# A table of rank corrections for the first part's order, and a buffer of its own for the second chunk's q

## The chip, the cores and the metric

The kernel runs on one core of one Trainium2 chip. The metric is the time of one execution on the device in microseconds (us); of several runs the median counts.

## The reference, cut to what matters

Attention over keys and values that are averaged in groups of 8, for 8 batches of 576 tokens and 8 heads of 64, and behind it a feed-forward net with a softplus on all 4608 tokens. The weights arrive as float64.

```python
k_p = k.reshape(B, H, S // 8, 8, D).mean(axis=3)
v_p = v.reshape(B, H, S // 8, 8, D).mean(axis=3)
scores = (q @ k_p.transpose(0, 1, 3, 2)) / sqrt(D)
attn = exp(scores - max(scores)); attn = attn / (sum(attn) + 1e-9)
x = (attn @ v_p).transpose(0, 2, 1, 3).reshape(4608, 512)
h = x @ w_in                                  # 512 -> 2048
out = (max(h, 0) + log1p(exp(-abs(h)))) @ w_out
```

## The kernel before

The 4608 tokens are cut into 18 chunks of 256 (two tiles of 128). Each matrix of the feed-forward net is used as a high and a low part (three products for one) on TensorE (PE). w_in and w_out are cut into 16 slices; slice f of both becomes one weight, w0 to w15, which VectorE (DVE) and ScalarE (ACT) convert from the float64 bits.

The program has two parts. The first makes the pooled keys and values of batches 0 and 1 (and 2 for later), converts the 16 weights, does the attention of chunks 0 to 3, and runs chunks 0 to 2 through the net. The second part does the other chunks in a steady pattern, from chunk 4 on with a product scheme that needs fewer products (its operands are the combined w_out, written to DRAM and loaded again by `load_sums`).

In each part the order is planned before anything is issued. Every step is an `Op` with an engine, a cost, the steps that it comes after, and `Slot`s, the buffers that it uses. `Order.run` walks through time: on the engine that could be done first it picks, of the ready steps, the one with the highest rank plus `first`, a correction given with the step. The rank is the cost of the longest chain of steps behind it. Each of the engines then runs its steps strictly in the planned order; a step whose input is late holds all behind it. SyncE (SP) issues all the transfers in one such queue.

Names in what follows: `kps` are the products that pool the keys, `kvlp` those of the last eight keys and values of a batch that don't fill a group of 64, `vps` those of the values; `qTp` transposes q, `sc` are scores, `mn` their minima (keys are scaled by a negative number), `sm` sums, `pm` and `pe` the normalised probabilities (main part and ends), `ptp` and `ltp` their transpositions, `avp` the products with the values. `wst` is a raw slice of w_in or w_out, `wg` a slice in conversion; the conversion is five steps on DVE, a cast on ACT, and a last subtraction on DVE that writes w. `h` are the products with w_in, `acc` and `m` those with w_out.

Chunks 0, 1 and 2 share one memory for q: a tile of chunk 1 can only be loaded when PE has transposed the same tile of chunk 0. `LD` names four load buffers for keys, values and late weights. `spin` hands out tags of a list in turn, whatever slot the plan chose, and the pool `two` alternates on its own for `mn` and `sm`:

```python
def spin(tags, shape, dtype, name):
    tags.append(tags.pop(0))
    return one.tile(shape, dtype, tag=tags[-1], name=name)
...
o_q.append(op(SYNC, 1.4, load,
              [] if c == 0 else [q_free[c - 1, t]] if c < N1 else
              [q_free[c - 1, i] for i in range(T)], lag=2.4))
```

Of the kernel before, what the change touches and what calls it, by code (L numbers as in the profile page):

```python
# [9 lines left out]
F32 = mybir.dt.float32  # L10
# [93 lines left out]
def pooled_attention_softplus_ffn(  # L104
# [41 lines left out]
    def spin(tags, shape, dtype, name):  # L146

        tags.append(tags.pop(0))
        return one.tile(shape, dtype, tag=tags[-1], name=name)

# [90 lines left out]
    def kv(b):  # L241
# [9 lines left out]
        def k_pool(i):  # L251
            if i == 0:
                kp.append(one.tile([SP, H, D], F32, tag="kp", name="kp"))
            tree(st_.pop(("k", i)), kp[0][:, 2 * i:2 * i + 2], engine)
# [7 lines left out]
        def v_pool(i):  # L262
            if i == 0:
                vp.append(one.tile([P, HP, D], F32, tag="vp", name="vp"))
            tree(st_.pop(("v", i)), vp[0][:, 2 * i:2 * i + 2], engine)
# [63 lines left out]
    class Tile:  # L329
# [29 lines left out]

        def least(self, j, ps):  # L360
# [15 lines left out]

        def exp_sum(self, j, ps):
            if j == 0:
                self.sm = two.tile([P, H], F32, tag="sm", name="sm")
# [6 lines left out]
        def sum(self):  # L386
            self.sm = two.tile([P, H], F32, tag="sm", name="sm")
            nc.vector.tensor_reduce(out=self.sm, in_=e_[self.c][:, self.t], axis=AX.X, op=ALU.add)
# [11 lines left out]
        def ends(self):  # L400

            pe = one.tile([P, 7 * R], F32, tag="pe", name="pe")
            self.pe = pe[:, 0:6 * R].rearrange("p (a n r) -> p a n r", a=2, n=3)
# [114 lines left out]

    def copy_out(c, t, tag=None):
        o = one.tile([P, DM], F32, tag=tag, name="o") if tag else spin(O, [P, DM], F32, "o")  # L520
# [186 lines left out]
    def load_wi(c, u):  # L707

        for k in range(2):
# [5 lines left out]

    kinds = {"bank": BANKS, "ld": LD, "ct": ["T0"], "kv": "a", "wg": "ab", "o": "ab", "qT": "ab", "mn": "ab",
             "sm": "ab", "E0": "a", "E1": "a", "pm": "a", "pe": "a", "kp": "a", "vp": "a", "lt_": "a",
             "pT": "a", "g": ["G0", "G1"], "gh": "ab", "gl": "ab", "h": "ab", **{x: "a" for x in late[:NS]}}
# [23 lines left out]
    def weights(f):  # L742
# [5 lines left out]
        def load(i):  # L748
            def fn():
                if early:  # L750
                    if not i:
                        x["raw"] = wpool.tile([P, 2, 4 * 2 * P], I32, tag=late[f % NS], name="wst")
                    st = x["raw"][:, i]
                else:
                    st = x["raw", i] = one.tile([P, 4 * 2 * P], I32, tag=stages[i].name, name="wst")
                if i:
                    nc.sync.dma_start(out=st, in_=wo32[f * P:(f + 1) * P, :])
                else:
                    for r in range(2):
# [4 lines left out]
            return op(SYNC, 1.75, fn, slots=[stages[0 if early else i]], lag=2.2)  # L764

# [16 lines left out]
        def bits(k):  # L782
# [5 lines left out]
            else:  # L788
                g = x["g", k] = spin(O, [P, 1, 4 * P], I32, "wg")
                up = x["raw", k].unsqueeze(1).rearrange("p x (n w) -> p x n w", w=2)[:, :, :, 1]  # L790
# [56 lines left out]
    def batch(b):  # L847
# [24 lines left out]
        o_left = op(SYNC, 1.3, load_left, slots=[ld], lag=2.2)  # L872
        o_k = [op(SYNC, 1.75, load(k, i), slots=[st[i]], lag=2.2) for i in range(2)]
        o_v = [op(SYNC, 1.75, load(v, i), slots=[vt[i] or vt[0]], lag=2.2) for i in range(2)]

# [74 lines left out]
    def attend(c):  # L950
        s_lt, s_pT = Slot("lt_"), Slot("pT")
        lows, e_c = [], []
        tiles = [Tile(c, t) for t in range(T)]
        o_q, subs = [], []
        for t in range(T):
            def load(t=t):
                if 0 < c < N1:
                    qt_[c] = qt_[0]
                elif c not in qt_:
                    new_q(c)  # L960
                load_q_tile(c, t)
            o_q.append(op(SYNC, 1.4, load,
                          [] if c == 0 else [q_free[c - 1, t]] if c < N1 else
                          [q_free[c - 1, i] for i in range(T)], lag=2.4))
        norms = []
        for t, x in enumerate(tiles):
# [5 lines left out]
            o = op(PE, 0.5, lambda x=x, s=s_q: x.qT(bank(s, "qTp")),  # L972
                   [o_q[t], *([av[c - 1]] if c == N1 else [])], [s_q])
            q_free[c, t] = o
            o = op(ACT, act(512), lambda x=x, s=s_q: x.qT_out(s.tile), [o], [s_q, s_qT])
            ends, ss = [], [Slot("bank"), Slot("bank")]
# [3 lines left out]
            for i, s in enumerate(ss):  # L980
                d = op(DVE, 0.46, lambda x=x, i=i, s=s: x.least(i, s.tile), [p, *ends],
                       [s, s_mn])
                if c < N1:
                    def exp_sum(x=x, i=i, s=s, e=s_E[0], t=t):
# [4 lines left out]
                        x.exp_sum(i, s.tile)  # L989
                    ends.append(op(ACT, 1.2, exp_sum, [d], [s, s_mn, s_sm, *s_E], table="exp"))  # L990
# [13 lines left out]
        for x, ends, s_E, s_sm, s_pm, s_pe in norms:  # L1004
            if c == N1:
                ends = [op(DVE, 0.75, x.sum, [ex], [s_sm])]
            o = op(DVE, 1.45, x.norm, ends, [*s_E, s_sm, s_pm, s_pe])
# [21 lines left out]
    def feed(c):  # L1029
# [21 lines left out]
        if c < N1 - 1:  # L1051
            for t in range(T):
                s = Slot("o")
                h = {}

                def copy(t=t, h=h):
                    h["o"] = copy_out(c, t)
                o = op(DVE if t % 2 else ACT, 0.65, copy, [before2], [s, acc_slots[c][t]])
# [73 lines left out]
    for u in range(U1):  # L1132
        combinations(u)
    with tc.manual_schedule(engines={ACT, DVE, PE, SYNC}):
        for o in todo.run():
            o.fn()
# [6 lines left out]
    kinds = {"h": other[:2], "acc": other[2:4], "bank": other[4:], "ld": LD, "q": "a", "pT": "a", "qT": "ab", "lt_": "a",  # L1143
             "pe": "a", "mn": "ab", "sm": "ab", "E": "a", "kp": "a", "vp": "a", "S": "ab", "x": "b",
# [16 lines left out]
    def steady_attention(c):  # L1161
# [8 lines left out]
        for x in tiles:  # L1170
# [4 lines left out]
            qT_done[c].append(o)  # L1175
            o = op(ACT, act(512), lambda x=x, s=s: x.qT_out(s.tile), [o], [s, s_qT])
            last, ss = [], [Slot("bank"), Slot("bank")]
# [3 lines left out]
            for i, s in enumerate(ss):  # L1181
                last = [op(DVE, 0.46, lambda x=x, i=i, s=s: x.least(i, s.tile), [p, *last],
                           [s, s_mn])]
# [8 lines left out]
    def probabilities(c, tiles, s_E, s_lt, subs, where):  # L1192
# [4 lines left out]
        for x in tiles:  # L1197
            s_sm, s_pm, s_pe = Slot("sm"), Slot("G"), Slot("pe")
            o = op(DVE, 0.76, x.sum, [ex], [s_E, s_sm])
            o = op(DVE, 0.38, x.reciprocal, [o], [s_sm])  # L1200
# [189 lines left out]
```

## Time and profile before

| | us |
|---|---|
| median of 3 runs (lowest, highest) | 928.23 (927.97, 931.43) |
| the profiled execution | 930.85 |
| its span, first to last instruction | 929.1 |
| PE busy in the span | 904.6 (97%) |
| DVE busy | 648.6 (70%) |
| ACT busy | 407.3 (44%) |

Busy is the time in which an engine executes at least one instruction. Idle time of an engine counts only where another waits for it. The DMA share is the mean busy share of the core's 16 DMA engines. PEclk is the granted clock of PE as a share of the full one: 1.00 or 0.50, with means between where a stretch holds both.

### The profile page before, as it was taken

What the parts mean: (1) busy time and instruction counts of PE and PEld (TensorE: products, weight loads), DVE (VectorE), ACT (ScalarE), POOL (GpSimd) and SP (SyncE); (2) the same over time, 40 slices, a digit from 0 to 9 for tenths busy, and PEclk for the clock granted to TensorE, in tenths of its full rate; (3) what the DMA queues carried; (4) which work ended last, traced back from release to release, by engine and by line L of the source; (5) the groups of instructions that cost most, each with busy time, mean ns of one, the idle gap of its engine ahead of it and who ended that gap; (6) DMA issues with size and microseconds to landing.
All of it is one profiled execution on the core that took longest, in us unless ns stands there. A gap on an engine that the chain in (4) does not pass through costs nothing.

```text
span 929.1 us, 20504 instructions
## 1 busy us (share of the span) xinstructions
PE 904.6 (97%) x8304; PEld 859.6 (93%) x8304; DVE 648.6 (70%) x1600; ACT 407.3 (44%) x824; POOL 2.4 (0%) x19
## 2 busy tenths in 40 slices
PE   4899999999999999999999999999999999999997
PEld 2678989889899999999999999999999999999997
DVE  4799988868876767777777755777666565747454
ACT  4755433344443534544453435353535344434332
POOL 1000000000000000000000000000000000000000
PEclk9899999999999999999999999999999999999999
DMA  8974636544898678788668865777656566647472
GB/s 231 259 249 147 205 106 182 167 150 136 289 276 239 225 212 256 201 248 233 224 198 248 238 208 186 212 245 214 220 172 216 182 206 186 222 141 227 158 238 78
DMA packets 107085, 191.12 MB, mean 206 GB/s; under 512 B 46064, under 2 KB 60400, under 8 KB 106992
## 3 DMA queue, kind: packets, MB, share of 16 engines
q1 hardware_dynamic: 106992, 189.82, 66.2%
q8 instruction: 65, 1.06, 0.5%
q14 instruction: 28, 0.23, 0.1%
HBM read 167.25 MB, written 22.54 MB: 204 GB/s over the span
## 4 chain that ended last, share of the span: by engine, by line
PE 93%; DVE 3%; DMA 3%; ACT 0%; issue 0%; SPq 0%; DVEq 0%; ACTq 0%
PE h L494 43%; PE m L684 30%; PE acc L516 7%; PE sc L357 3%; PE acc L576 2%; PE avp L461 2%; PE qTp L337 2%; PE avp L468 1%; PE ptp L420 1%; DMA vst<-in_v_dram 1%; PE ltp L432 1%; PE kps L921 1%; DMA kvst<-in_k_dram 1%; DMA kvl<-in_v_dram 1%; DMA wst<-in_moe_w_in_dram 0%
## 5 line engine op out<-in xcount | busy, mean ns | idle before, releaser
L494 PE MATMUL h<-x,w 128*128 128x256 f32 x3456 | 437.8, 282 | 0.7 <-DVE w L822 0.7
L494 PEld LDWEIGHTS h<-x,w 128*128 128x128 f32 x3456 | 422.5, 188 | 4.0 <-DVE w L822 0.9
L543 ACT ACTIVATE g<-h 128x512 f32<-128x512 f32 x120 | 71.7, 598 | 287.0 <-PE h L494 284.7
L684 PE MATMUL m<-w,so 128*128 128x256 f32 x1344 | 177.7, 281 | 0.0
L684 PEld LDWEIGHTS m<-w,so 128*128 128x128 f32 x1344 | 167.4, 188 | 0.0
L684 PE MATMUL m<-w,gh 128*128 128x256 f32 x672 | 133.4, 288 | 0.0
L594 DVE TENSOR_TENSOR sf<-g 128x128 f32<-128x128 f32 x112 | 32.7, 292 | 141.1 <-ACT g L543 140.0
L684 PEld LDWEIGHTS m<-w,gh 128*128 128x128 f32 x672 | 102.2, 188 | 1.9
L684 PE MATMUL m<-w,gl 128*128 128x256 f32 x336 | 94.1, 280 | 0.0
L608 ACT CAST so<-sf 128x512 fp32r<-128x512 f32 x112 | 69.6, 621 | 55.1 <-DVE sf L597 54.6
L613 DVE TENSOR_TENSOR so<-sf,so 128x512 fp32r<-128x512 f32 x112 | 77.3, 690 | 21.9 <-ACT so L608 21.8
L564 DVE TENSOR_TENSOR gl<-g,gh 128x384 fp32r<-128x384 f32 (+1 forms) x120 | 67.3, 560 | 0.7 <-ACT gh L557 0.5
L684 PEld LDWEIGHTS m<-w,gl 128*128 128x128 f32 x336 | 63.1, 188 | 0.0
L516 PE MATMUL acc<-w,g 128*128 128x512 f32 x192 | 60.7, 397 | 0.5 <-ACT g L499 0.5
L557 ACT ACTIVATE gh<-h 128x384 fp32r<-128x384 f32 (+1 forms) x120 | 59.3, 494 | 0.0
L499 ACT ACTIVATE g<-h 128x256 fp32r<-128x256 f32 x96 | 31.6, 382 | 60.7 <-PE h L494 55.6
L705 DVE TENSOR_TENSOR o<-o,m 128x256 f32<-128x256 f32 x98 | 39.7, 418 | 3.9 <-ACT o L697 1.0
L516 PEld LDWEIGHTS acc<-w,g 128*128 128x128 f32 x192 | 34.2, 189 | 6.6 <-ACT g L499 0.7
L364 DVE TENSOR_REDUCE mn<-sc 128x4 f32<-128x288 f32 x72 | 31.1, 450 | 12.2 <-PE sc L357 12.1
L516 PE MATMUL acc<-w,gl 128*128 128x512 f32 x96 | 38.0, 396 | 0.0
L597 DVE TENSOR_TENSOR sf<-g,sf 128x128 f32<-128x128 f32 x112 | 32.7, 292 | 3.9
L406 DVE TENSOR_TENSOR pe<-E,sm 128x96 f32<-128x96 f32 x72 | 15.2, 252 | 26.9 <-PE ltp L432 26.9
(165 smaller groups left out, 933.0 us busy)
## 6 DMA issues: line engine op xcount, KB each, us to landing
w<-wi SPq DMA_DIRECT2D x224, 512.0 KB
out_dram<-o SPq DMA_DIRECT2D x36, 256.0 KB
q<-in_q_dram SPq DMA_DIRECT2D x32, 256.0 KB
wst<-in_moe_w_in_dram SPq DMA_DIRECT2D x32, 256.0 KB
wst<-in_moe_w_out_dram SPq DMA_DIRECT2D x16, 512.0 KB
wi<-w SPq DMA_DIRECT2D x16, 512.0 KB
kst<-in_k_dram SPq DMA_DIRECT2D x24, 288.0 KB
vst<-in_v_dram SPq DMA_DIRECT2D x24, 256.0 KB
```

Source lines behind the costliest of these rows:

```text
L494: nc.tensor.matmul(out=ps[:, 0:CT], lhsT=row(w, kc), rhs=x[:, kc], start=first and kc == j == 0, stop=last and kc == KC - 1 and j == 2)
L499: nc.scalar.activation(out=g, in_=ps[:, 0:CT], func=AF.Softplus)
L516: nc.tensor.matmul(out=accs[c][t], lhsT=a[:, ts], rhs=w, start=f == 0 and j == 0, stop=f == FC - 1 and j == 2)
L543: nc.scalar.activation(out=g, in_=x.rearrange("p (b i) -> p b i", i=P), func=AF.Softplus)
L557: nc.scalar.activation(out=gh, in_=quarters(c, x.rearrange("p (b i) -> p b i", i=P)), func=AF.Softplus)
L564: nc.vector.tensor_tensor(out=gl, in0=quarters(c, g), in1=gh.bitcast(F32), op=ALU.subtract)
L594: tt(out=sf[:, 2], in0=g[:, 0], in1=g[:, 2], op=ALU.add)
L597: tt(out=sf[:, 3], in0=g[:, 3], in1=sf[:, 1], op=ALU.subtract)
L608: nc.scalar.copy(out=so[:, 0], in_=ss[c, u])
L613: nc.vector.tensor_tensor(out=so[:, 1], in0=sf, in1=so[:, 0].bitcast(F32), op=ALU.subtract)
L684: nc.tensor.matmul(out=ms[c][n], lhsT=x, rhs=y, start=u == 0 and j == 0 and n in (1, 6, 5, 4), stop=u == FP - 1 and j == 2 and n in (2, 7, ...
L705: nc.vector.tensor_tensor(out=o, in0=in0, in1=m[n], op=how)
```

## The change

It does four things. The second chunk's q gets one of the four load buffers (slot `s_q1`), held from its load to its transposition; the third chunk uses the first chunk's memory again and waits only for that. The buffers of q's transpositions, outputs, minima and sums take the tag that the plan chose; `spin` and the pool `two` go. In the first part the planner starts with SP at 0.8 and the exponential table loaded, and some loads cost 1.5 instead of 1.75. And a table, `HASTE`, adds a correction to `first` of 110 of the first part's 647 steps, by their number. In the second part the loads of the combined w_out lose their extra rank of 500.

```diff
-    two = ctx.enter_context(tc.tile_pool(name="two", bufs=2))
...
-        def qT_out(self, ps):
-            self.q = spin(Q, [P, HP, P], F32, "qT")
+        def qT_out(self, ps, tag):
+            self.q = one.tile([P, HP, P], F32, tag=tag, name="qT")
...
-                self.mn = two.tile([P, 2, HP], F32, tag="mn", name="mn")
+                self.mn = one.tile([P, 2, HP], F32, tag="mn" + tag, name="mn")
...
+    todo.begin, todo.table = {SYNC: 0.8}, "exp"
...
-        o_k = [op(SYNC, 1.75, load(k, i), slots=[st[i]], lag=2.2) for i in range(2)]
+        o_k = [op(SYNC, 1.5, load(k, i), slots=[st[i]], lag=2.2) for i in range(2)]
...
-        o_q, subs = [], []
+        o_q, subs, s_q1 = [], [], Slot("ld")
...
-                if 0 < c < N1:
+                if c == 1 and c not in qt_:
+                    qt_[c] = one.tile([P, T, H, D], F32, tag=s_q1.name, name="q")
+                elif c == 2:
                     qt_[c] = qt_[0]
...
-                          [] if c == 0 else [q_free[c - 1, t]] if c < N1 else
-                          [q_free[c - 1, i] for i in range(T)], lag=2.4))
+                          [] if c < 2 else [q_free[0, t]] if c < N1 else
+                          [q_free[c - 1, i] for i in range(T)], [s_q1] if c == 1 else [], lag=2.4))
...
+    HASTE = {27: -130, 29: -3, 34: -120, 36: -120, 45: 40, 46: 20, 48: -180, 55: -2, 56: -10,
...
+    for i, x in HASTE.items():
+        todo.ops[i].first += x
...
-               lag=2.4, first=500))
+               lag=2.4))
```

What the plan makes of it, at three places. First SP's queue behind the first chunk's q: transfers in the order of issue, with what an issue waits for (an engine, or, as DMAHW, an earlier transfer). Before, q_143 is the memory shared by the chunks:

```order
L760 DMA wst_152<-in_moe_w_in_dram 128x2x256 x2
L308 DMA q_143<-in_q_dram 128x8x64 [waits DMAHW4_49,DMAHW0_49,PE_49]
L308 DMA q_143<-in_q_dram 128x8x64 [waits DMAHW5_49,DMAHW1_49,PE_49]
L757 DMA wst_152<-in_moe_w_out_dram 128x1024 [waits DMAHW2_49]
L867 DMA kvst_238<-in_k_dram 128x4x256 [waits DMAHW3_49]
L867 DMA kvst_251<-in_v_dram 128x4x256 x2
```

Now, where q_139 is the memory of chunks 0 and 2 and q_237 that of chunk 1:

```order
L753 DMA wst_149<-in_moe_w_in_dram 128x2x256 x2
L750 DMA wst_149<-in_moe_w_out_dram 128x1024 [waits DMAHW0_49]
L302 DMA q_139<-in_q_dram 128x8x64 [waits DMAHW5_49,DMAHW1_49,PE_49]
L860 DMA kvst_225<-in_k_dram 128x4x256 [waits DMAHW2_49]
L302 DMA q_237<-in_q_dram 128x8x64 [waits DMAHW3_49,DVE_49]
L302 DMA q_237<-in_q_dram 128x8x64 [waits DMAHW4_49]
```

The w_out slice has moved ahead of the waits for PE, one tile of chunk 2 stands where two of chunk 1 stood, and chunk 1's two tiles stand behind the keys of batch 1.

Second PE's queue behind the first chunk's scores, down to batch 1's kvlp. Before:

```order
L337 MATMUL qTp<-ident,q 128x128 x8
L921 MATMUL kps<-kvst,zm 64x256 x4
L357 MATMUL sc<-kT_94,qT 64x72 x32
L432 MATMUL ltp<-ident,pe 96x128 x2
L938 MATMUL vps<-kvst,zm 64x128 x16
L921 MATMUL kps<-kvst,zm 64x256 x4
L880 MATMUL kvlp<-kvl,zl 72x512
```

Now, from the same kps on (one qTp of four stands ahead of it):

```order
L914 MATMUL kps<-kvst,zm 64x256 x4
L331 MATMUL qTp<-ident,q 128x128 x8
L351 MATMUL sc<-kT_91,qT 64x72 x16
L424 MATMUL ltp<-ident,pe 96x128 x2
L412 MATMUL ptp<-ident,pm 128x128 x4
L351 MATMUL sc<-kT_91,qT 64x72 x16
L931 MATMUL vps<-kvst,zm 64x128 x16
L424 MATMUL ltp<-ident,pe 96x128 x2
L412 MATMUL ptp<-ident,pm 128x128 x4
L914 MATMUL kps<-kvst,zm 64x256 x4
L331 MATMUL qTp<-ident,q 128x128 x4
L873 MATMUL kvlp<-kvl,zl 72x512
```

Chunk 1's transpositions of q have moved behind kps; both tiles' ltp and ptp of chunk 0 and one more qTp now stand ahead of kvlp. The value products of chunk 0 (avp), which stood behind the scores of chunk 2's first tile, follow right behind this kvlp.

Third DVE's queue down to its copy of batch 1's last keys (`COPY kp`). Before:

```order
L364 TENSOR_REDUCE mn<-sc 128x4 x2
L808 SCALAR_TENSOR_TENSOR wg<-wst,wg 128x1024
L444 TENSOR_TENSOR lt__355<-ltp,lt__355 32x2x128
L813 SCALAR_TENSOR_TENSOR wg<-wst,wg 128x1024
L364 TENSOR_REDUCE mn<-sc 128x4
L889 COPY kp<-kvlp 8x512
```

Now:

```order
L358 TENSOR_REDUCE mn<-sc 128x4
L815 TENSOR_TENSOR w_261<-wg,w_261 128x2x512
L358 TENSOR_REDUCE mn<-sc 128x4
L436 TENSOR_TENSOR lt__353<-ltp,lt__353 32x2x128
L386 TENSOR_SCALAR sm<-sm 128x8
L387 RECIPROCAL sm<-sm 128x8
L391 TENSOR_TENSOR pm<-E,sm 128x512
L398 TENSOR_TENSOR pe<-E,sm 128x96 x2
L882 COPY kp<-kvlp 8x512
```

All of weight 0's conversion (w_261 is w0; its five steps stand further ahead) and three normalisations (rows sm, sm, pm, pe; two of them not shown) are now ahead of the copy; before, one normalisation was, and the last step of weight 0 came later.

## Rows read from the trace of the kernel before

**Rows 1.** The page's opening line.

```profile
span 929.1 us, 20504 instructions
```

**Rows 2.** Busy time by stages: busy us of each engine, granted clock, DMA share, GB/s.

```profile
14.80:34.00 19.20, 13.95 (x140) 9.69 (x140) 11.39 (x24) 11.56 (x57) 0.00 (x0) 0.82 0.92 246
34.00:82.00 48.00, 41.60 (x432) 34.97 (x433) 44.02 (x90) 33.41 (x98) 0.00 (x0) 0.96 0.73 231
82.00:179.00 97.00, 97.00 (x624) 88.07 (x623) 85.90 (x149) 35.79 (x89) 0.00 (x0) 1.00 0.52 165
179.00:300.00 121.00, 120.23 (x1041) 110.28 (x1040) 90.95 (x211) 54.97 (x103) 0.00 (x0) 1.00 0.70 220
300.00:924.20 624.20, 624.01 (x5991) 612.50 (x5990) 410.52 (x1119) 267.47 (x474) 0.00 (x0) 1.00 0.67 207
```

(The busy times are those of PE, PE's weight loads, DVE, ACT and POOL, in this order.)

**Rows 3.** Timeline of PE: start, duration, work, [idle before, released by].

```profile
15.38 0.63 PE L337 MATMUL qTp<-ident,q 128*128 128x128 f32 x4 [0.58 <-DVE mn L364]
17.66 0.63 PE L337 MATMUL qTp<-ident,q 128*128 128x128 f32 x4 [1.66 <-DMA q<-in_q_dram]
20.69 3.64 PE L921 MATMUL kps<-kvst,zm 128*64 128x256 f32 x8 [2.40 <-DMA kvst<-in_k_dram]
```

**Rows 4.** Timeline of SP's queue: start and duration of the issues.

```profile
6.10 1.73 SPq L760 DMA_DIRECT2D wst<-in_moe_w_in_dram  x2
12.24 1.54 SPq L308 DMA_DIRECT2D q<-in_q_dram  x2
13.84 0.57 SPq L757 DMA_DIRECT2D wst<-in_moe_w_out_dram  x1
14.46 0.42 SPq L867 DMA_DIRECT2D kvst<-in_k_dram  x1
```

**Rows 5.** Timeline of DVE.

```profile
18.84 0.69 DVE L791 TENSOR_SCALAR wg<-wst 128x1024 int32<-128x1024 int32 x1 [2.00 <-DMA wst<-in_moe_w_out_dram]
...
20.18 0.16 DVE L392 TENSOR_SCALAR sm<-sm 128x8 f32<-128x8 f32 x1
...
21.22 0.42 DVE L406 TENSOR_TENSOR pe<-E,sm 128x96 f32<-128x96 f32 x2
...
25.54 0.46 DVE L364 TENSOR_REDUCE mn<-sc 128x4 f32<-128x288 f32 x1 [3.29 <-PE sc L357]
...
31.86 0.69 DVE L889 COPY kp<-kvlp 8x512 f32<-8x512 f32 x1 [1.51 <-PE kvlp L880]
...
38.22 1.22 DVE L822 TENSOR_TENSOR w<-wg,w 128x1024 fp32r<-128x1024 f32 x1
```

**Rows 6.** Timeline of PE, 32 to 79 us.

```profile
32.09 1.04 PE L337 MATMUL qTp<-ident,q 128*128 128x128 f32 x8
...
36.56 0.76 PE L357 MATMUL sc<-kT,qT 64*64 64x72 f32 x27 [1.37 <-ACT kT L225]
...
37.21 1.94 PE L461 MATMUL avp<-pT,vs 64*64 64x256 f32 x15
...
43.01 0.40 PE L432 MATMUL ltp<-ident,pe 128*96 128x128 f32 x2 [1.21 <-DVE pe L406]
...
51.74 0.40 PE L432 MATMUL ltp<-ident,pe 128*96 128x128 f32 x2 [1.44 <-DVE pe L406]
...
78.08 0.40 PE L432 MATMUL ltp<-ident,pe 128*96 128x128 f32 x2 [1.46 <-DVE pe L406]
```

**Rows 7.** Busy time by stages, short stretches (columns as in rows 2).

```profile
20.00:22.00 2.00, 1.31 (x4) 0.75 (x5) 1.93 (x7) 1.08 (x4) 0.00 (x0) 0.50 1.09 359
20.70:26.70 6.00, 6.00 (x74) 3.82 (x74) 2.14 (x6) 0.99 (x6) 0.00 (x0) 0.50 1.19 269
37.00:40.40 3.40, 3.40 (x42) 2.42 (x36) 3.00 (x5) 3.34 (x19) 0.00 (x0) 0.50 1.02 334
```

**Rows 8.** Batch 1's values: timelines of SP's queue and of PE.

```profile
34.20 1.58 SPq L867 DMA_DIRECT2D kvst<-in_v_dram  x2
...
43.77 2.57 PE L938 MATMUL vps<-kvst,zm 128*64 128x128 f32 x32
```

More of the change, by code (lines that the diff above doesn't have):

```diff
@@ L251, in k_pool @@
         def k_pool(i):
-            if i == 0:
+            if not kp:
                 kp.append(one.tile([SP, H, D], F32, tag="kp", name="kp"))
@@ L375, in less, with exp_sum @@
                     [P, 2, 2, SP]), op=ALU.subtract)
-        def exp_sum(self, j, ps):
+        def exp_sum(self, j, ps, tag):
             if j == 0:
-                self.sm = two.tile([P, H], F32, tag="sm", name="sm")
+                self.sm = one.tile([P, H], F32, tag="sm" + tag, name="sm")
             for m in range(HP):
@@ L384, in exp_sum, with sum @@
                                      accum_out=self.sm[:, h:h + 1])
-        def sum(self):
-            self.sm = two.tile([P, H], F32, tag="sm", name="sm")
+        def sum(self, tag):
+            self.sm = one.tile([P, H], F32, tag="sm" + tag, name="sm")
             nc.vector.tensor_reduce(out=self.sm, in_=e_[self.c][:, self.t], axis=AX.X, op=ALU.add)
@@ L400, in ends @@
         def ends(self):
-            pe = one.tile([P, 7 * R], F32, tag="pe", name="pe")
-            self.pe = pe[:, 0:6 * R].rearrange("p (a n r) -> p a n r", a=2, n=3)
+            self.pe = one.tile([P, 2, 3, R], F32, tag="pe", name="pe")
             for a in range(2):
@@ L517, in ffn2, with copy_out @@
                                  start=f == 0 and j == 0, stop=f == FC - 1 and j == 2)
-    def copy_out(c, t, tag=None):
-        o = one.tile([P, DM], F32, tag=tag, name="o") if tag else spin(O, [P, DM], F32, "o")
+    def copy_out(c, t, tag):
+        o = one.tile([P, DM], F32, tag=tag, name="o")
         if t % 2 == 0:
@@ L763, in fn @@
                                 "(g r p) f -> r p g f", r=2, p=P)[r])
-            return op(SYNC, 1.75, fn, slots=[stages[0 if early else i]], lag=2.2)
+            return op(SYNC, 1.5, fn, slots=[stages[0 if early else i]], lag=2.2)
         loads = [load(i) for i in range(2)]
@@ L788, in bits @@
             else:
-                g = x["g", k] = spin(O, [P, 1, 4 * P], I32, "wg")
+                g = x["g", k] = one.tile([P, 1, 4 * P], I32, tag=gslot[k].name, name="wg")
                 up = x["raw", k].unsqueeze(1).rearrange("p x (n w) -> p x n w", w=2)[:, :, :, 1]
@@ L872, in batch @@
         o_left = op(SYNC, 1.3, load_left, slots=[ld], lag=2.2)
-        o_k = [op(SYNC, 1.75, load(k, i), slots=[st[i]], lag=2.2) for i in range(2)]
-        o_v = [op(SYNC, 1.75, load(v, i), slots=[vt[i] or vt[0]], lag=2.2) for i in range(2)]
+        o_k = [op(SYNC, 1.5, load(k, i), slots=[st[i]], lag=2.2) for i in range(2)]
+        o_v = [op(SYNC, 1.5, load(v, i), slots=[vt[i] or vt[0]], lag=2.2) for i in range(2)]
         s_left, s_kp, s_vp = Slot("bank"), Slot("kp"), Slot("vp")
@@ L972, in attend @@
             o = op(PE, 0.5, lambda x=x, s=s_q: x.qT(bank(s, "qTp")),
-                   [o_q[t], *([av[c - 1]] if c == N1 else [])], [s_q])
+                   [o_q[t], *([av[c - 1]] if c == N1 else [])], [s_q, *([s_q1] if c == 1 else [])])
             q_free[c, t] = o
-            o = op(ACT, act(512), lambda x=x, s=s_q: x.qT_out(s.tile), [o], [s_q, s_qT])
+            o = op(ACT, act(512), lambda x=x, s=s_q, n=s_qT: x.qT_out(s.tile, n.name), [o], [s_q, s_qT])
             ends, ss = [], [Slot("bank"), Slot("bank")]
@@ L980, in attend, with exp_sum @@
             for i, s in enumerate(ss):
-                d = op(DVE, 0.46, lambda x=x, i=i, s=s: x.least(i, s.tile), [p, *ends],
+                d = op(DVE, 0.46, lambda x=x, i=i, s=s, n=s_mn: x.least(i, s.tile, n.name), [p, *ends],
                        [s, s_mn])
                 if c < N1:
-                    def exp_sum(x=x, i=i, s=s, e=s_E[0], t=t):
+                    def exp_sum(x=x, i=i, s=s, e=s_E[0], t=t, n=s_sm):
                         if c == 0 and 0 not in e_:
@@ L988, in exp_sum @@
                         x.slot = e.name
-                        x.exp_sum(i, s.tile)
+                        x.exp_sum(i, s.tile, n.name)
                     ends.append(op(ACT, 1.2, exp_sum, [d], [s, s_mn, s_sm, *s_E], table="exp"))
@@ L1005, in attend @@
             if c == N1:
-                ends = [op(DVE, 0.75, x.sum, [ex], [s_sm])]
+                ends = [op(DVE, 0.75, lambda x=x, n=s_sm: x.sum(n.name), [ex], [s_sm])]
             o = op(DVE, 1.45, x.norm, ends, [*s_E, s_sm, s_pm, s_pe])
@@ L1054, in feed, with copy @@
                 h = {}
-                def copy(t=t, h=h):
-                    h["o"] = copy_out(c, t)
+                def copy(t=t, h=h, s=s):
+                    h["o"] = copy_out(c, t, s.name)
                 o = op(DVE if t % 2 else ACT, 0.65, copy, [before2], [s, acc_slots[c][t]])
@@ L1175, in steady_attention @@
             qT_done[c].append(o)
-            o = op(ACT, act(512), lambda x=x, s=s: x.qT_out(s.tile), [o], [s, s_qT])
+            o = op(ACT, act(512), lambda x=x, s=s, n=s_qT: x.qT_out(s.tile, n.name),
+                   [o], [s, s_qT])
             last, ss = [], [Slot("bank"), Slot("bank")]
@@ L1181, in steady_attention @@
             for i, s in enumerate(ss):
-                last = [op(DVE, 0.46, lambda x=x, i=i, s=s: x.least(i, s.tile), [p, *last],
+                last = [op(DVE, 0.46, lambda x=x, i=i, s=s, n=s_mn: x.least(i, s.tile, n.name), [p, *last],
                            [s, s_mn])]
@@ L1198, in probabilities @@
             s_sm, s_pm, s_pe = Slot("sm"), Slot("G"), Slot("pe")
-            o = op(DVE, 0.76, x.sum, [ex], [s_E, s_sm])
+            o = op(DVE, 0.76, lambda x=x, n=s_sm: x.sum(n.name), [ex], [s_E, s_sm])
             o = op(DVE, 0.38, x.reciprocal, [o], [s_sm])
```

11 lines of the change are left out of this document (4 added, 7 removed), and 12 rows, old and new, of the table HASTE.

## The prediction

> **What bounds the kernel now.** I read the page's opening line first, then the busy time by stages, since a share over the whole span hides where time is lost. [rows 1, 2] The span is 929.1 us. From 82 to 179 us PE is busy 97.00 of 97.00 us, and from 300 to 924.2 us 624.01 of 624.20: there nothing but less PE work would help, and the change leaves the number of PE's instructions as it is. What can be won lies ahead of 82 us: from 14.8 to 34 PE is busy 13.95 of 19.20 us, from 34 to 82 41.60 of 48.00, idle 5.25 and 6.40.
>
> The second view is the timeline of PE and, for who is late, of SP and DVE. PE's scores of the first chunk end at 14.80 (15.38 less the 0.58 of idle time). Then it waits 0.58, 1.66 and 2.40 us, and only at 20.69 do the products of the second batch's keys (kps) start [rows 3]. The last two waits are for transfers. SP shows why: it is free at 7.83, but stands until 12.24, because its next two loads write the second chunk's q over the first chunk's and must wait for PE's transpositions; the w_out half of the first weight and the keys queue behind, at 13.84 and 14.46 [rows 4]. DVE in turn waits for that w_out until 18.84, then 3.29 us for scores [rows 5]. In 14.8 to 34 it is busy only 11.39 of 19.20 us; from 34 to 82 it is at work 44.02 of 48.00 [rows 2], and PE's idle pieces there end mostly on it: 1.21, 1.44, 1.46 us for DVE's pe; 1.37 is for the keys that ACT scales [rows 6]. So DVE leaves time unused early and has none later.
>
> The third view is the granted clock in short stretches. After the 4.64 us of waits PE runs at 0.50 from 20.7 to 26.7, and once more from 37 to 40.4, behind 1.37 us of waiting [rows 7]. PE is fully busy in both, so half of 6.0 and of 3.4 us is lost: 3.0 and 1.7. The Trainium skill (TensorE: Matmul & The Clock Gate, section "What's actually happening") has two levels, 1.2 and 2.4 GHz, idle sending PE to the lower and busy work back; the rows agree.
>
> **The change, part by part.** *The start of the queue.* With a buffer of its own the second chunk's q needn't wait for the first's transpositions. In the new order the w_out half goes out right behind w_in, at 7.9 rather than 13.84, into a queue that was empty. One q tile still waits for PE (a tile of the third chunk, which does overwrite); the old pair of such loads was out by 13.78 [rows 4], so this one is too, and the key half stands right behind: 13.85 instead of 14.46, 0.6 earlier. Ahead of it in the transfers are 0.75 MB less (one q tile of 0.25 MB, the w_out half of 0.5 MB); at the 359 GB/s of 20 to 22 us [rows 7] that is 2.1 us. Together 2.7, so kps could start at 18.0. Against it: PE has then transposed one q tile where it had two, half of the 1.04 us of eight such [rows 6], so the lead in work is 2.2; and the scores behind kps now wait for ACT's copy of a tile transposed only just before. No row has that wait; its bounds are 0 and the 0.58 of PE's own small wait at 15.38 [rows 3]; I take 0.3, nearer to the middle since the second tile's transposition lies over part of it. **(a) 1.9 us**; bounds 0.3 (if the transfers gain nothing but SP's 0.6, less 0.3) and 2.2.
>
> *The clock.* PE's idle stretch ahead of kps shrinks from 4.64 to some 3 us. Whether that spares it the first slow stretch no row shows: between 0 and 3.0. I take 0.6, near nothing, because the longest wait stays long. The second stretch came behind the 1.37 us; the new order puts the first chunk's value products, 1.94 us of them in the slow stretch [rows 6], ahead of those scores instead of behind them, so PE has work while ACT is late. I take all 1.7; bounds 0 and 1.7. **(b) 2.3 us.** At full clock throughout, (b) would be 4.7.
>
> *The table.* It moves work between stages on DVE and PE. At the row where DVE copies the second batch's left-over keys (31.86 before, released by PE's kvlp [rows 5]), the new order has ahead of it two more normalisations, one more minimum and the last step of weight 0. A normalisation runs from 20.18 to 21.64, 1.46 us; the minimum is 0.46, the last step 1.22 [rows 5]: 2 x 1.46 + 0.46 + 1.22 = 4.6 us. PE has eight more qTp, eight ptp (the same form) and two ltp ahead of that kvlp: 1.04 + 1.04 + 0.26 = 2.3 us [rows 6]. With a lead of 1.9 + 0.6 = 2.5, PE reaches kvlp at about the old time, and by then DVE is 4.6 us ahead of its old self. That is possible, since it idled 7.8 us in 14.8 to 34; what makes it possible is the w_out that lands while DVE has nothing else.
>
> From 34 to 82 PE lives on what DVE hands it. PE's lead, (a) plus (b), is 4.2; DVE's 4.6 carries it and leaves 0.4. On top the order may close part of DVE's own 3.98 idle us there; the bounds are nothing and all of it. I take a third, 1.3, because the same engine hands work back and forth with ACT and PE and every hand-over can make a new wait. **(c) 1.7 us**; bounds 0, and the 6.40 that PE idles.
>
> *What costs nothing.* Pools replaced by tags, the smaller pe tile, and names bound at planning add no instruction. A wait that the old rotation of buffers could have caused beyond 300 us would show as PE idle, and there is 0.19 us of it. The loads of the combined w_out lose their rank and fall a few rows back in SP's queue; they are hidden by PE's full queue (179 to 300: 120.23 of 121.00 busy), and if that cover were gone each would cost PE a transfer's delay. The correction of SP's start and of the load costs only shifts the plan.
>
> **Sum.** 1.9 + 2.3 + 1.7 = 5.9 us. The profiled execution took 930.85 (span 929.1, 1.75 around it), 2.62 above the median of 928.23. So I expect 924.95 for one like the profiled one, and for the median 922.3, 0.64% less. What this kernel's measurement can tell from no change is about 0.5%, 4.6 us; below 923.6 counts as faster.
>
> **Rivals.** *The transfers stay the bound.* In 14.8 to 34 the DMA share is 0.92 [rows 2]: moving one load forward moves another back. For it: SP's loads from 14.46 on are the same bytes. Against it: the empty stretch from 7.83 to 12.24. Then only (a) remains and waits reappear later: 926.3. Chance 0.16.
>
> *The clock falls as before.* (b) is gone, 928.2 - 3.6 = 924.6. For it: a wait of some 3 us stays ahead of kps. The same page of the Trainium skill says that the gate runs free of the kernel's start, so the point at which it falls differs from run to run; by that rule one trace can't promise (b), and the time would be this one. Chance 0.10.
>
> *More than that.* DVE's lead also removes the waits in its name, and PE stays at full clock: 1.9 + 4.7 + 5.0 of the 6.40 = 11.6, 916.6. Against it: the new order has its own hand-overs. Chance 0.12, spread from 916 to 920.
>
> *Slower: the second batch's values come late.* The second chunk's q takes one of four load buffers, so those values wait for a buffer, and the second half stands behind the fourth chunk's q, which waits for PE. In the old order they were out by 35.78 and used at 43.77 without a wait, at most 8.0 us [rows 8]. In the new order their last issue comes after PE's qTp beside kvlp, about 32.5, landing by 40.5; PE gets there at about 39.5. A us of lateness costs one, since all behind stands in PE's order: 1 us is likely harmless within (c), landing at 45.4 uses up the gain, at 50.0 the kernel is slower by 0.5%. Chance 0.06 for no gain or a loss (930 to 934).
>
> **Numbers.** The forecast's case, 920.0 to 924.7, has 0.56, of which 0.46 below 923.6. The range 919.0 to 927.0 leaves out part of the first and third rivals and all of the fourth, about 0.19. Faster: 0.46 + 0.12 = 0.58. Same: 0.10 + 0.16 + 0.10 + 0.01 = 0.37. Slower: 0.05.
>
> **What would show it.** In the new trace kps of the second batch starts near 18.0, not 20.7; DVE starts weight 0 near 15; the granted clock has one slow stretch, not two; the first product with weight 0 (right behind the values' products, which end at 46.34 before [rows 8]) starts between 41.5 and 43; PE's idle from 34 to 82 is about 3.5 us; from 82 on it is full. I'm wrong if kps starts after 20, if the values of the second batch hold PE, or if PE's busy stretch after 82 has new holes.

## The result and the profile after

The changed kernel took 920.6 us (median of 4 runs, 919.36 to 922.68), the kernel before 928.88 in the same measurement (4 runs, 927.97 to 931.43): a ratio of 0.9909, interval 0.9879 to 0.9938. In the two later groups of runs, in which each kernel ran more often, the kernel before had 930.12 (16 runs, 927.52 to 935.84) and 930.77 (21 runs, 927.73 to 935.71), the changed kernel 919.88 (6 runs, 919.24 to 921.73) and 919.59 (5 runs, 919.2 to 921.84): ratios of 0.9878 [0.9844, 0.9912] and 0.9871 [0.9852, 0.989]. So the gain is 8.3 us by the first measurement and 10.2 and 11.2 by the larger ones. In these the changed kernel's runs also lie closer together, 2.5 and 2.6 us apart instead of 8.3 and 8.0, though they are fewer; in the first, with four runs each, it was 3.3 and 3.5.

The opening line of its page and its busy time by stages, as in [rows 1, 2]:

```profile
span 920.9 us, 20496 instructions
```

```profile
14.80:34.00 19.20, 15.76 (x170) 10.57 (x162) 14.66 (x33) 16.03 (x75) 0.00 (x0) 0.82 0.99 260
34.00:82.00 48.00, 45.76 (x466) 38.92 (x459) 45.09 (x88) 30.72 (x86) 0.00 (x0) 1.00 0.73 231
82.00:179.00 97.00, 97.00 (x628) 87.17 (x627) 90.02 (x158) 37.59 (x89) 0.00 (x0) 1.00 0.53 176
179.00:300.00 121.00, 121.00 (x1081) 112.84 (x1080) 91.84 (x217) 54.16 (x102) 0.00 (x0) 1.00 0.70 218
300.00:916.00 616.00, 616.00 (x5903) 604.92 (x5901) 402.69 (x1097) 265.42 (x470) 0.00 (x0) 1.00 0.68 208
```

PE idles 3.44 us from 14.8 to 34 (5.25 before), 2.24 from 34 to 82 (6.40 before), and not at all from 82 to 916, where it had 0.77 and 0.19 [rows 2]. That is 1.81 + 4.16 + 0.96 = 6.9 us. PE's busy time as a whole fell by another 1.1 us, from 904.6 to 903.5. Together 8.0 of the 8.2 between the two spans.

Its timeline of PE, SP's queue and DVE at the places of [rows 3 to 6, 8]:

```profile
16.71 0.63 PE L331 MATMUL qTp<-ident,q 128*128 128x128 f32 x4 [1.74 <-DMA q<-in_q_dram]
19.04 3.64 PE L914 MATMUL kps<-kvst,zm 128*64 128x256 f32 x8 [1.71 <-DMA kvst<-in_k_dram]
...
36.45 0.72 PE L351 MATMUL sc<-kT,qT 64*64 64x72 f32 x30 [0.23 <-ACT kT L219]
37.80 0.40 PE L424 MATMUL ltp<-ident,pe 128*96 128x128 f32 x2 [0.62 <-DVE pe L398]
...
40.32 2.57 PE L931 MATMUL vps<-kvst,zm 128*64 128x128 f32 x32
42.82 1.68 PE L486 MATMUL h<-x,w 128*128 128x256 f32 x12
```

```profile
7.86 0.47 SPq L750 DMA_DIRECT2D wst<-in_moe_w_out_dram  x1
13.49 0.37 SPq L302 DMA_DIRECT2D q<-in_q_dram  x1
13.91 0.58 SPq L860 DMA_DIRECT2D kvst<-in_k_dram  x1
...
33.55 2.51 SPq L860 DMA_DIRECT2D kvst<-in_v_dram  x1
```

```profile
15.39 0.68 DVE L784 TENSOR_SCALAR wg<-wst 128x1024 int32<-128x1024 int32 x1
...
28.48 1.23 DVE L815 TENSOR_TENSOR w<-wg,w 128x1024 fp32r<-128x1024 f32 x1
```

The w_out half goes out at 7.86 instead of 13.84, and DVE begins weight 0 at 15.39 instead of 18.84 and ends it at 29.7 instead of 39.4 [rows 4, 5]. The waits of 1.2 to 1.5 us for DVE's pe are down to 0.62 and less. The values of the second batch are there when PE comes to them (no bracket at 40.32).

The granted clock, stretches that answer to [rows 7]:

```profile
17.80:24.20 6.40, 5.16 (x16) 3.23 (x16) 4.65 (x9) 3.74 (x18) 0.00 (x0) 0.50 1.08 297
36.00:41.00 5.00, 3.67 (x78) 2.74 (x80) 4.83 (x13) 3.56 (x15) 0.00 (x0) 1.00 0.88 249
```

One slow stretch is left of two.

How far PE is ahead by then can be read at one row that all the kernels have: the first product m (of the scheme that is used from chunk 4 on). In the kernel before, and in the changed one:

```profile
258.14 0.40 PE L684 MATMUL m<-w,gh 128*128 128x256 f32 x2
```

```profile
251.09 0.40 PE L676 MATMUL m<-w,gh 128*128 128x256 f32 x2
```

So 7.05 of the 8.2 us are won ahead of this row. In the two later profiles of the changed kernel it stands at 249.90 and 250.25.

### The profile page after: what moved, and what is told of

The parts are those of the page before. It is cut to its first block, busy times and chain, and to the rows that moved or that the text cites. A ratio compares the mean times of both kernels' runs of the same rounds, so it can differ in the third digit from the quotient of the medians.

```text
span 920.9 us, 20496 instructions
## 1 busy us (share of the span) xinstructions
PE 903.5 (98%) x8304; PEld 858.8 (93%) x8304; DVE 649.9 (71%) x1600; ACT 407.8 (44%) x824; POOL 2.4 (0%) x19
## 4 chain that ended last, share of the span: by engine, by line
PE 95%; DVE 2%; DMA 1%; SPq 1%; ACT 0%; issue 0%; DVEq 0%; ACTq 0%
PE h L486 44%; PE m L676 31%; PE acc L508 7%; PE acc L568 2%; PE sc L351 2%; PE avp L453 2%; PE qTp L331 2%; PE ptp L412 1%; PE avp L460 1%; DMA wst<-in_moe_w_out_dram 1%; PE ltp L424 1%; DMA kvl<-in_v_dram 1%; SPq L302 0%; ACT E L376 0%; DVE o L697 0%; DVE wg L806 0%
```

## The experiments

Three groups, each with the kernel before on the same chip. In the first the kernel before took 930.23 (17 runs), nearly as in the other two, so its times can be set beside the 919.6 to 919.9 of the changed kernel, which did not run in it.

**Without the table.**

```diff
-    for i, x in HASTE.items():
-        todo.ops[i].first += x
```

> The changed kernel without the table of corrections; the second chunk's own buffer for q, the named buffers and the planner's new costs stay. Theory A (most of the 8 us comes from the new order on DVE and PE from 34 us on, of which the table is the cause): most of the gain goes, ratio to the kernel before 0.996 to 1.000, PE idle from 34 to 82 us 5 us or more. Rival B (the gain is the earlier start of the queue, which the buffer alone gives): ratio 0.991 to 0.994.

929.48 us (12 runs), ratio 0.999 [0.9976, 1.0004]: the whole gain is gone. But the profile doesn't show it where the table was thought to work. The stages 34 to 82 and 179 to 300, and PE's waits in the second:

```profile
34.00:82.00 48.00, 44.13 (x441) 37.30 (x433) 44.71 (x86) 31.05 (x88) 0.00 (x0) 1.00 0.70 228
...
179.00:300.00 121.00, 117.02 (x1017) 108.00 (x1015) 88.34 (x207) 53.82 (x100) 0.00 (x0) 1.00 0.72 217
```

```profile
286.49 0.66 PE L331 MATMUL qTp<-ident,q 128*128 128x128 f32 x4 [0.72 <-DVE x L470]
287.69 0.66 PE L331 MATMUL qTp<-ident,q 128*128 128x128 f32 x4 [0.54 <-DVE x L470]
299.85 1.08 PE L351 MATMUL sc<-kT,qT 64*64 64x72 f32 x32 [2.19 <-DVE E L365]
```

In 14.8 to 82 us PE idles 4.83 + 3.87 = 8.7, three us less than before (3.87 from 34 to 82, where 5 or more were expected); in 179 to 300 it idles 4.0, three more. Its first m stands at 253.43, 4.7 us ahead of the kernel before, and at the end only 1.5 of them are left (span 927.6). The size came as expected and the reason did not.

The plan shows how the table reaches so far: the second part is planned from the state in which the first ends. Without the table the second part's order on PE, DVE and ACT is step for step that of the kernel before; with it, 21 of PE's 415 places and 55 of SP's 209 hold another step.

**The second chunk's q in shared memory again**, with the table kept and the plan made anew:

```diff
-                if c == 1 and c not in qt_:
-                    qt_[c] = one.tile([P, T, H, D], F32, tag=s_q1.name, name="q")
-                elif c == 2:
+                if 0 < c < N1:
                     qt_[c] = qt_[0]
...
```

> The changed kernel with the table, but the second chunk's q again in the first chunk's memory; the plan is made anew with the same table. Theory A: the start of the queue is lost (about 2 us, the keys of the second batch after 20 us) and what the table does later stays in part, ratio 0.994 to 0.998. Rival B: nothing is left without the buffer, ratio 0.998 to 1.002.

924.83 us (6 runs), 0.9942 [0.9927, 0.9956], as expected: 5 us over the changed kernel. The products of the second batch's keys start at 20.41, behind three waits for transfers (1.04, 1.75, 2.13), nearly as in [rows 3]; from 179 to 300 us PE doesn't wait. The w_out half goes out late too, at 13.28, and DVE starts weight 0 at 18.87, so the 5 us are not the keys' alone.

**The w_out half late**: on SP behind the second chunk's q, and DVE's first steps of weight 0 behind its minima; all else as changed.

```diff
+    behind(41, 269)      # SP: weight 0's w_out half behind the second chunk's q
+    behind(42, 249)      # DVE: its first step behind a minimum
...
+    behind(43, 42)
```

> The changed kernel's order, with one transfer later: the w_out half of the first weight is issued behind the keys and the second chunk's q, as late as in the kernel before, and DVE's first two steps on that weight stand behind the scores' minima. Everything else keeps its place. Theory A (DVE's lead, made by a w_out that lands while DVE has nothing else): DVE starts the weight at 18 to 20 us instead of 15.4, PE idles 3 to 5 us more before 60 us, ratio 0.994 to 0.997. Rival B (the keys' arrival and the clock): less than 0.6 us, ratio 0.990 to 0.992.

926.12 us (6 runs), 0.9952 [0.9937, 0.9967], as expected: 6 us over the changed kernel. PE's timeline shows the price, DVE late by the work that it could not do early:

```profile
27.23 0.66 PE L424 MATMUL ltp<-ident,pe 128*96 128x128 f32 x2 [3.95 <-DVE pe L398]
```

But the edit does more than take the lead away. The half is issued at 15.21 and DVE starts weight 0 later than in the kernel before (18.84) and than the 18 to 20 us that were expected:

```profile
21.30 0.69 DVE L784 TENSOR_SCALAR wg<-wst 128x1024 int32<-128x1024 int32 x1 [5.89 <-DMA wst<-in_moe_w_out_dram]
```

The normalisation that PE waits for stands behind all five steps on this weight, in an order made for an early w_out, and the granted clock from 14.8 to 34 us is 0.73 where it was 0.82. So 6 us is what this order loses without the early transfer, and not what the lead gives over the kernel before.

**The rank of the loads put back** (one of the edits costed at nothing):

```diff
-               lag=2.4))
+               lag=2.4, first=500))
```

> The changed kernel with the old rank of 500 for the loads of the combined w_out in the second part. All theories so far: within 0.5 us of the changed kernel, ratio 0.990 to 0.992. If the 0.8 us of PE's idle time that went away between 179 and 300 us is this edit's, 0.8 us slower than the changed kernel and that idle time is back.

925.1 us (6 runs), 0.9941 [0.9925, 0.9956]: a miss, 5 us. The rank changes more than SP's queue here: the plan of the second part comes out otherwise on PE (45 of 415 places), DVE and ACT too. Its profile has a hole in the stretch that the prediction took as full, and SP's queue says why:

```profile
253.57 3.08 PE L486 MATMUL h<-x,w 128*128 128x256 f32 x24 [2.77 <-DMA w<-wi]
```

```profile
245.55 1.02 SPq L520 DMA_DIRECT2D out_dram<-o  x2
246.68 0.94 SPq L657 DMA_DIRECT2D w<-t  x2
247.68 1.86 SPq L704 DMA_DIRECT2D w<-wi  x4
249.58 2.01 SPq L242 DMA_DIRECT2D kst<-in_k_dram  x2
```

The slices of w_in for that product go out at 247.68, behind loads of the combined w_out (`w<-t`); the changed kernel has a pair of them out here:

```profile
244.94 1.04 SPq L704 DMA_DIRECT2D w<-wi  x2
```

**The changed kernel again, and three edits beside it.** Its measure in this group:

> The changed kernel once more, as the measure for the other three of this group. Every theory expects 920 to 923 us, a ratio of 0.990 to 0.993.

919.88 us, as told above. The first edit keeps PE's clock up by extra transposes in the two waits for transfers:

```diff
+            for _ in range(14 if (self.c, self.t) == (2, 1) else 0):
+                nc.tensor.transpose(out=ps[:, 0:P], in_=ident, identity=ident)
...
+                for _ in range((0, 13)[b] if i == 0 else 0):
+                    nc.tensor.transpose(out=bank(s_k, "kps")[:, 0:P], in_=ident, identity=ident)
```

> The changed kernel with 14 extra transposes ahead of the transposes of the second chunk's second q tile, and 13 ahead of the second key/value batch's first pooled product, written into the same PSUM tiles and overwritten; they fill the two waits of 1.74 and 1.71 us for transfers. Nothing of the computation is left out. Theory C (the slow stretch of TensorE's clock that follows these waits still costs the changed kernel 1 to 2.5 us): the stretch is gone and the time is 1 to 2.5 us under the changed kernel's. Rival (what PE does there hangs on ACT's and DVE's hand-overs, not on its own speed): within 0.6 us of the changed kernel, and the waits for ACT and DVE behind it grow by what PE saves.

921.05 us (6 runs), 0.9884 [0.985, 0.9918], no better than 919.88. The clock did stay up; 16 to 34 us here:

```profile
16.00:34.00 18.00, 16.14 (x181) 11.48 (x180) 13.93 (x32) 15.27 (x69) 0.00 (x0) 1.00 1.03 278
```

against this in the unedited kernel of the same group:

```profile
16.00:34.00 18.00, 16.74 (x161) 11.32 (x162) 13.69 (x31) 15.03 (x68) 0.00 (x0) 0.81 1.04 271
```

The waits have moved rather than gone: one of 0.79 us for q appears at 30.70, and the keys' products wait 0.75 where they waited 0.57. At the first m 0.6 us is left (249.32 against 249.90). The run doesn't price the clock, since the extra transposes are 3.3 us of PE's time themselves (1.75 and 1.58).

The second puts the first half of the second batch's keys ahead of chunk 2's q tile, on SP and PE. (The expectation names two tiles; the edit passes one.)

```diff
+    ahead(23, 302)       # SP: first half of batch 1's keys ahead of chunk 2's q tile
+    ahead(33, 310)       # PE: its products ahead of that tile's transposes
```

> The changed kernel with one more step of the start put forward: on SP the first half of the second batch's keys ahead of the second chunk's second and third q tiles, and on PE the pooled product of these keys ahead of those tiles' transposes. If the wait for these keys is a loss of its own (step (a) of the prediction, us for us): the pooled product starts 1 to 3 us earlier and the time falls by 1.5 to 3 us. Rival (the q tiles come as much later, and ACT and DVE, which work on their scores, wait instead): within 0.7 us of the changed kernel.

920.75 us (6 runs), 0.9888 [0.9856, 0.992], no gain, though its PE timeline has the products 3.4 to 4.1 us earlier than the profiles of the changed kernel, and without a wait:

```profile
14.90 1.94 PE L914 MATMUL kps<-kvst,zm 128*64 128x256 f32 x8
17.06 0.63 PE L331 MATMUL qTp<-ident,q 128*128 128x128 f32 x4 [0.22 <-DVE wg L789]
18.25 0.63 PE L331 MATMUL qTp<-ident,q 128*128 128x128 f32 x4 [0.56 <-DMA q<-in_q_dram]
19.23 0.63 PE L331 MATMUL qTp<-ident,q 128*128 128x128 f32 x4 [0.36 <-DMA q<-in_q_dram]
21.65 1.24 PE L351 MATMUL sc<-kT,qT 64*64 64x72 f32 x32 [1.78 <-ACT qT L338]
```

The wait has moved to DVE's, q's and ACT's names, as the rival said, and the first m stands at 249.91, where it did.

The third is the rank's removal alone, in the kernel before (the diff of the rank above, the other way round):

> The kernel before with one edit of the change alone: the rank of 500 taken from the loads of combined w_out; 22 rows move in SP's queue, none on PE, DVE or ACT. If that rank costs by itself the 3 us that the run with the rank put back into the changed kernel lost: 926 to 927 us, a ratio of 0.996 to 0.998. Rival (it costs only with the list that the planner makes behind the new first part, where a slice of w_in comes late): as the kernel before, within 0.6 us, a ratio of 0.9993 to 1.0007.

931.66 us (12 runs, 927.76 to 936.14), 1.0009 [0.9988, 1.003]: by itself it is worth nothing, the rival's case. The profiled execution was the longest of the twelve, 936.14 us, and gave the clue to the rest. Up to 285 us it stands where the kernel before stands; then DVE waits for a key and two value loads of the fourth batch, and PE for DVE:

```profile
287.30 1.14 DVE L212 TENSOR_TENSOR kst<-kst 72x512 f32<-72x512 f32 x2 [2.77 <-DMA kst<-in_k_dram]
294.23 1.15 DVE L212 TENSOR_TENSOR vst<-vst 128x512 f32<-128x512 f32 x2 [2.14 <-DMA vst<-in_v_dram]
300.02 1.15 DVE L212 TENSOR_TENSOR vst<-vst 128x512 f32<-128x512 f32 x2 [4.32 <-DMA vst<-in_v_dram]
```

```profile
305.11 1.08 PE L357 MATMUL sc<-kT,qT 64*64 64x72 f32 x32 [2.98 <-DVE E L371]
```

In the profiled execution of the kernel before, which was shorter, PE's wait at this place was 0.17. Behind the waits the clock falls once more:

```profile
306.50:309.90 3.40, 3.40 (x19) 3.40 (x18) 1.73 (x5) 0.89 (x2) 0.00 (x0) 0.50 0.50 146
```

PE's waits here are 3.9 us (0.39, 0.54 and 2.98) for 0.4 in the kernel before, and half of 3.4 us goes to the clock: 3.5 + 1.7 = 5.2 of the 5.3 us between the two spans (934.4 and 929.1). The two are different programs, but by the medians the edit between them is worth nothing, and both have runs from under 928 to some 936 us. So it is likely, though not shown on one program, that this place differs by 3 us and more between executions. It is also the one that undid the run without the table.

**Where the loads of the fourth batch stand.** That gave theory L: these loads land too late, and part of the gain is that the changed kernel's list has them earlier. Three edits touch SP's order alone, in the second part; the changed kernel ran beside them.

> The changed kernel once more, on the chip of the other three of this group, as their measure. Every theory expects 919 to 923 us, a ratio of 0.987 to 0.993.

919.59 us. First, the kernel before with these loads early:

```diff
+    ahead(305, 142)      # next chunk's q tile, eight slices of w_in earlier
+    ahead(274, 248)      # keys of the fourth batch, one pair earlier
+    ahead(278, 258)      # values, one pair earlier
+    ahead(280, 289)
```

> The kernel before with one edit in the second part, on SP alone: the next chunk's q tile eight w_in slices earlier, and of the fourth key/value batch one load of keys and both loads of values one pair of w_in slices earlier. No row moves on PE, DVE or ACT. Theory L (at 285 to 305 us these loads land too late for DVE and so for PE, by an amount that differs from run to run, and part of the change's gain is that its list places them earlier): PE's waits at 290 to 302 us are gone, the time is 1 to 3 us under the kernel before and its runs lie closer together. Rival (all of the gain lies in the first 82 us): within 0.7 us of the kernel before.

928.32 us (10 runs, 927.48 to 930.2), 0.9969 [0.9953, 0.9985]: 2.5 us less in the median, and no run is longer than 930.2; the shortest one is as before (927.48 and 927.73). So the edit takes away what the worse executions lose.

Not all of the 2.5 is the loads'. In its profile the first m stands at 255.86, 2.3 us ahead already, though the edit leaves the first part as it was: the second slow stretch of the clock is missing there. Behind this row it gains 0.5 more (span 926.3). Of its ten runs 7 have a mean granted clock of 0.996 or more, of the 21 of the kernel before 6. Among these the medians are 928.01 and 929.09, among the others 929.46 and 931.84: 1.1 to 2.4 us at a like clock.

The same four lines in the kernel without the table:

> The changed kernel without its table (as in the first group) and with the early loads. Without the table the profile showed PE idle for 8.7 us in 14.8 to 82 us, 3.0 us less than in the kernel before, and for 4.0 us in 179 to 300 us, 3.2 more, which cancelled. Theory L: the second of these goes, 925 to 927 us, a ratio of 0.994 to 0.997; what then is left to the changed kernel, 5 to 6 us, is what the table is worth in the first 82 us with what follows from it. Rival (the table alone carries the gain): 929 us, as without the table.

925.05 us (6 runs), 0.9928 [0.9911, 0.9945]: 4.4 us under the kernel without the table. Its first 82 us had been better all along, and the late loads had eaten it: the first m stands at 253.10, 5.0 us ahead of the kernel before, and at the end it is 5.7 (span 923.4), where 4.7 had become 1.5.

Last, the changed kernel with the loads where the kernel before has them:

```diff
+    ahead(305, 248)
+    ahead(274, 258)
+    ahead(278, 289)
```

> The changed kernel with the opposite edit, on SP alone: the same q tile and the same loads of the fourth batch put back to the places that they have in the kernel before, between the same w_in slices. Theory L: PE waits 0.4 to 4 us for DVE or ACT at 275 to 300 us, and the time is 1 to 4 us over the changed kernel. Rival: within 0.7 us of it.

928.42 us (12 runs, 923.4 to 931.28), 0.9964 [0.9946, 0.9983]: 8.8 us over the changed kernel, more than twice the most that was expected. Of the three loads two change their place among the slices of w_in, the next chunk's q tile and the first values of the fourth batch; the keys come out where they stood. So four fifths of the gain hang on the places of two loads in SP's queue; nothing else differs. The execution with a profile was the shortest of the twelve; of the others there is no trace. Even it shows DVE late by these values, PE's wait for DVE, and the stretch around it with the DMA engines full (share 1.03):

```profile
280.30 1.16 DVE L206 TENSOR_TENSOR vst<-vst 128x512 f32<-128x512 f32 x2 [2.59 <-DMA vst<-in_v_dram]
```

```profile
283.95 0.66 PE L331 MATMUL qTp<-ident,q 128*128 128x128 f32 x4 [1.75 <-DVE x L470]
```

```profile
265.00:285.00 20.00, 18.25 (x161) 17.39 (x161) 14.71 (x40) 7.92 (x16) 0.00 (x0) 1.00 1.03 259
```

The kernel before and then the changed kernel in the same stretch:

```profile
265.00:285.00 20.00, 20.00 (x172) 20.00 (x171) 14.42 (x40) 10.74 (x17) 0.00 (x0) 1.00 0.96 273
```

```profile
265.00:285.00 20.00, 20.00 (x179) 19.36 (x178) 15.67 (x41) 8.69 (x17) 0.00 (x0) 1.00 0.94 253
```

Its first m stands at 249.88, so the lead was there, and 0.8 us of it is lost behind it (span 921.7). The other runs must lose far more. Part of it may be the clock: at the medians their mean granted clock is 0.994, the changed kernel's in this group 1.000. A stretch like the one behind the waits of the rank alone, 3.4 us at half, takes 0.002 off such a mean, so by estimate it would be about three such stretches more, 5 us. Where they lie no trace shows.

In group 3 the chain is then: 930.77 before; 928.32 with its loads early; 925.05 with the change's other edits but no table; 919.59 with the table and the list that follows from it. That is 2.5, 3.3 and 5.5 us. The three are worth this in this order; they aren't independent, and some of the first is the clock, as told above.

## Why the prediction was right, and where it was not

The time (920.6 for a forecast of 922.3) lies in the range; the gain was 8.3 us in that measurement, and 10.2 and 11.2 in the larger ones, where the sum had 5.9. Most of the marks that were to show it did: DVE starts weight 0 at 15.39 (near 15), one slow stretch of the clock instead of two, the first product with weight 0 at 42.82 (41.5 to 43), the values without a wait, full from 82 us on. That this early gain was kept is luck as far as the prediction goes: it hung on two loads of the second part, which the prediction doesn't name. Step by step:

(a), *the start of the queue*: the keys' products start at 19.04, 18.32 and 18.66 in the three profiles of the changed kernel, 1.65 to 2.4 us earlier, for a forecast of 18.0 and 2.7. The mechanism is the one described, SP's empty stretch. But that a still earlier start is worth its own length is refuted for the changed kernel: with the products at 14.90 the time didn't fall. What sharing the memory costs (5 us, the second experiment) is more than (a); there DVE's start on weight 0 is late as well (18.87), so that run doesn't price (a) alone.

(b), *the clock*: reckoned as in the prediction, half of PE's busy time at 0.50, 5.16 / 2 = 2.6 us is left of 4.7, a saving of 2.1 where 2.3 was put. PE's busy time as a whole fell by 1.1. The run with the rank put back shows what the stretch that is left costs: its first part is that of the changed kernel, step for step, and its profile has the full clock there.

```profile
14.80:34.00 19.20, 15.46 (x174) 10.87 (x174) 16.28 (x37) 17.28 (x79) 0.00 (x0) 1.00 1.15 286
```

```profile
248.16 0.40 PE L676 MATMUL m<-w,gh 128*128 128x256 f32 x2
```

This first m is 1.7 to 2.9 us ahead of the three profiles of the changed kernel. In the 15 runs of the changed kernel the time goes the same way: the four with a mean granted clock of 0.995 or 0.996 took 921.6 to 922.68 us, ten of the others 919.2 to 919.91, one 921.84. So the size in the sum was sound. What it had wrong is to count on it: how much of a run is slow differs from execution to execution (a mean granted clock of 0.991 to 0.998 in the runs of the kernel before). The kernel before with its loads early has the same first part as the kernel before, and its profile has a clock of 1.00 from 34 to 82 us, where that of the kernel before has 0.96. The Trainium skill (TensorE: Matmul & The Clock Gate, "What's actually happening") has it that the gate isn't tied to the kernel's start, and these two profiles agree. The prediction gave that a rival's chance and took all of the second stretch into the sum.

(c), *the table and DVE's lead*: the mis-sized term. PE's idle time from 34 to 82 us was to fall from 6.40 to some 3.5 and fell to 2.24, and 1.81 us went from the stage before it; the sum had 1.7 for all that DVE would give. From the first product with weight 0 to the first m the lead over the kernel before grows by 3.6 us, in each of the three profiles of the changed kernel. That the new order lives on DVE's early work is shown by the third experiment: with a late w_out it loses 6 us and has one wait of 3.95 for DVE. That run overstates what the lead is worth, as told there.

*What costs nothing*: the step that failed. The prediction took the second part's order as given but for the rank. But the second part is planned behind the first, so its order changed with the table, and 8.8 us hang on two of its loads. The prediction read 120.23 of 121.00 us busy in [rows 2] as cover for the second part's loads. It named the price if the cover went, a transfer's delay to PE, and that is what putting the rank back cost, 2.77 us in the trace and 5 in the median. For the kernel before it was right: there the rank's removal changed nothing (1.0009). The cover was thin: the same row has a DMA share of 0.70, a mean over 121 us that hides 20 us at 0.96, and it is one execution, which at 291 and 301 us happened to wait 0.24 and 0.17 us where that of the rank alone waited 3.9. PE's busy share said that nothing waits there now. It didn't say how near the transfers were to making it wait once PE arrives earlier.

The rivals: the values of the second batch were in time (refuted by the row at 40.32). *The clock falls as before* came half true: the first slow stretch is there (6.4 us at 0.50), the second isn't. *More than that* was nearer to the idle times above: DVE's waits went, though the clock didn't stay full. *The transfers stay the bound* was wrong for the changed kernel, and right without the table, 250 us later than the prediction looked.

What stays open: why the changed kernel's early part doesn't get shorter when the keys come 4 us earlier (ACT and DVE are named by the waits, but neither was made faster); which of the two loads counts for how much; and how the changed kernel with late loads comes to lose 8.8 us in the median: its only trace is of the shortest execution, with a wait of 1.75.

## What to carry to other kernels

A gain early in a kernel is kept only if what is loaded later comes in time for it: without the table PE came 4.7 us sooner to a stretch where the DMA engines were full and lost 3.2 of them there, and with a few loads moved forward it lost none. So read the DMA share in stretches of 20 us or less wherever PE is full, not only where it idles, before an edit of the load order is costed at nothing. And when a part is taken out and the time goes back, look in the trace where it was lost: here the number matched the theory and the place did not.

## What the runs showed of the hardware

How much the DMA engines move at full share goes with the size of the packets. The kernel before at 240 to 245 us, and at 275 to 295 us:

```profile
240.00:245.00 5.00, 5.00 (x47) 4.39 (x37) 4.60 (x11) 1.88 (x4) 0.00 (x0) 1.00 0.99 333
...
275.00:295.00 20.00, 19.76 (x177) 18.74 (x179) 13.18 (x35) 8.25 (x18) 0.00 (x0) 1.00 1.02 260
```

and the packets of the same two stretches:

```profile
DMA packets 454, 1.66 MB, mean 333 GB/s; under 512 B 48, under 2 KB 48, under 8 KB 454
```

```profile
DMA packets 4352, 5.20 MB, mean 260 GB/s; under 512 B 2931, under 2 KB 2931, under 8 KB 4350
```

With 11% of the packets under 512 B 333 GB/s, with 67% 260, at nearly the same share. The Trainium skill (DMA: Bandwidth & Descriptors, "Specifications") gives 512 B as the least for full rate; the rows go that way, though they don't measure the threshold. So it may matter what is moved out of a full stretch, and not only how many bytes; no run here separates the two. With the next chunk's q tile issued at 229.76 instead of 269.82, and the fourth batch's first values at 268.11 instead of 280.96, the stretch from 265 to 300 us has 2351 packets under 512 B instead of 4461, for 8.04 MB instead of 8.96, and the one from 225 to 262 has 2500 instead of 441.
